# Decay attention and a gated MLP on one core: identity columns beside the keys, mixing from PSUM, double weight pieces, GpSimd relieved, one written order for every engine

## The chip, the cores and the metric

The kernel runs on one core of a Trainium2 chip. The metric is the device time of one execution in microseconds (us). The engines are TensorE (PE for its matmuls, PEld for its weight loads), VectorE (DVE), ScalarE (ACT), GpSimd (POOL) and SyncE (SP, which here only issues DMAs). SBUF is the on-chip memory with 128 partitions, PSUM the one into which matmuls write.

## The reference, cut to what matters

Batch 4, 8 heads, 768 positions, 64 channels a head. The attention has no softmax; it decays by a factor per head and is computed in blocks of 64 positions with a running state. Its output, with the heads laid side by side as 512 channels, goes into a gated MLP whose inputs are mixed with the previous position's.

```python
for b in range(nb):
    sl = slice(b * block, (b + 1) * block)
    qb, kb, vb = (q[:, :, sl], k[:, :, sl], v[:, :, sl])
    intra = np.einsum('bhic,bhjc->bhij', qb, kb) * Dmask[None]
    intra = np.einsum('bhij,bhjd->bhid', intra, vb)
    inter = np.einsum('bhid,bhde->bhie', qb * lam_pow[None], kv_state)
    out[:, :, sl] = intra + inter
    kb_dec = kb * rev_pow[None]
    kv_state = lam_block[None, :, None, None] * kv_state + np.einsum('bhsd,bhse->bhde', kb_dec, vb)
...
xk = mu_k * x + (1.0 - mu_k) * x_prev
xr = mu_r * x + (1.0 - mu_r) * x_prev
k = np.maximum(xk @ w_k, 0.0)
v = k * k @ w_v
r = 1.0 / (1.0 + np.exp(-(xr @ w_r)))
return (r * v).astype(np.float32)
```

`Dmask[i, j]` is the decay to the power i - j (0 above the diagonal), `lam_pow[i]` its power i + 1, `rev_pow[j]` its power 63 - j, `lam_block` its power 64. The weights w_k (512 x 1024), w_v (1024 x 512) and w_r (512 x 512) come as float64.

## The kernel before, in words

The 768 positions are six tiles of 128, two blocks each (`eo` = 0, 1). Heads go in four pairs (`hp`, members `ab`). For each tile and pair:

- `load_hp` loads keys, queries, keys by position, and values, in six DMAs on SP's queue. Queries land in a tile that is zero outside two corners (`Qb`), so that one matmul over 128 rows gives the scores of both heads.
- `attn1` makes the scores (line 155), multiplies them by the decay table `Dt` into `mv` (line 159), and writes queries times `LP` (the decay's powers) into the other half of `mv` (line 172, half of it on DVE, half on GpSimd).
- `attn_state` scales the keys by position (line 182), multiplies them with the values into `u` (line 187) and updates the states, which stand beside the values in `VS` (lines 195 to 205).
- `attn2` multiplies `VS` and `mv` into `xp` (line 220): within-block part and state part in one product, channels on the partitions. ACT copies it to SBUF (line 223), with one column in front for the previous position.
- `prep` mixes it with the previous position, once for r (`which` 1), once for k (`which` 0), on ACT and DVE or ACT and GpSimd, and `split` cuts each mixture into a high part of reduced precision (ACT) and the rest (line 122, on DVE or GpSimd, by a letter in the order).

Each product of the MLP is three matmuls (high by high, high by low, low by high) of 512 columns: `r_slot` has 12 a pair for the four batches, `k_slot` 12 for each eighth of w_k's columns, `v_slot` 12 for half of a batch. A tile has 48 + 96 + 96 of them. `k_slot` then takes the positive part (ACT, line 274), squares it (any engine, line 278) and splits it; `v_slot` multiplies by the sigmoid (line 299) and stores. PSUM has four tiles for r, k and v in turn, two for scores, one for `u` and one for `xp`.

The weights are turned from float64 to two float32 parts on the chip, in 20 pieces of 512 columns: `stage_w` loads a piece, `conv_w` takes the high word's absolute value (ACT, line 139), clamps it (DVE or GpSimd, line 140), shifts it (line 141), ORs in the low word's top bits (line 142) and the sign (line 144), and splits the result. Its scratch tile has four buffers. All of this happens within tile 0.

Two strings set the order in which the steps are written down, `FIRST` for tile 0 and `LATER` for each further tile, whose attention steps belong to the next tile. Letters name steps (L load, A scores, U state, B values, x and y mixtures, R, K, V matmuls, S and C weights). A scheduler may then move the instructions of an engine against each other.

## Time and profile before

| | |
|---|---|
| Median of 3 runs | 468.01 us (465.6 to 468.74) |
| Profiled execution | 468.55 us, of which the span on the core 466.8 us |
| Busy, share of the span | PE 92%, PEld 75%, DVE 57%, ACT 49%, POOL 46% |
| Moved by DMA | 43.00 MB, mean 92 GB/s |
| PE's granted clock, mean | 0.973 |

The profile is of one execution. Busy time is what an engine spent in its instructions; the records of matmuls overlap, and the distance between two starts tells more than the length of one. A float32 matmul shows as two records, each with its own weight load. The chain of waits goes back from the last instruction to whatever released each one. A row of a group gives the output and inputs, the count, the busy time in us and the mean of one in ns, then the idle time of the engine before it.

### The profile page before, as it was taken

How to read it: one execution, taken by the hardware profiler on the slowest of the kernel's cores; microseconds unless marked ns; L12 is line 12 of the kernel's file. 1: busy time of each engine (PE TensorE's matmuls, PEld its weight loads, DVE VectorE, ACT ScalarE, POOL GpSimd, SP SyncE). 2: the span in 40 equal slices, each digit the busy share in tenths (PEclk: the TensorE clock that was granted, in tenths of full speed). 3: DMA queues.
4: the chain of work that ended last, by engine and by line, in shares of the span. 5: the costliest groups of instructions: out<-in, count | busy, mean ns of one | idle time of the engine just before them, and what ended most of it. 6: DMA issues, size and time to landing. Idle time of an engine off the chain costs nothing.

```text
span 466.8 us, 7757 instructions
## 1 busy us (share of the span) xinstructions
PE 430.7 (92%) x3000; PEld 347.8 (75%) x3000; DVE 267.7 (57%) x381; ACT 226.6 (49%) x396; POOL 214.9 (46%) x237
## 2 busy tenths in 40 slices
PE   2597869689889999999999999999999999999997
PEld 2465657567657888888888887888878888888886
DVE  4589999998896415728328546338463266132121
ACT  3376646555483546714546535457335456054410
POOL 4457858756376136925038533145523355121300
PEclk9997979889998999999999999999999999999999
DMA  8899554523123201324004342024142000100011
GB/s 176 241 302 269 162 166 148 165 81 120 72 68 114 70 0 47 112 91 138 22 1 123 104 131 75 22 53 130 67 151 54 0 25 2 69 23 0 1 45 46
DMA packets 22749, 43.00 MB, mean 92 GB/s; under 512 B 4536, under 2 KB 4792, under 8 KB 22712
## 3 DMA queue, kind: packets, MB, share of 16 engines
q1 hardware_dynamic: 19112, 36.20, 26.7%
q10 hardware_dynamic: 3600, 6.29, 3.6%
q8 instruction: 24, 0.39, 0.4%
q14 instruction: 13, 0.11, 0.1%
HBM read 36.19 MB, written 6.30 MB: 91 GB/s over the span
## 4 chain that ended last, share of the span: by engine, by line
PE 71%; DVE 16%; DMA 8%; issue 2%; ACT 2%; SPq 0%; POOL 0%; DVEq 0%; POOLq 0%
PE vp L295 24%; PE kp L271 24%; PE rp L258 12%; PE xp L220 4%; DVE wst L142 3%; PE sc L155 3%; PE u L187 3%; DVE wst L144 2%; DMA qb<-qT 2%; DVE wu L141 2%; DMA wst<-w_r 2%; DVE mv L172 2%; DVE mv L159 2%; DMA kn<-kN 1%; DMA kt<-kT 1%
## 5 line engine op out<-in xcount | busy, mean ns | idle before, releaser
L295 PE MATMUL vp<-wvh,k 128*128 128x512 f32 (+1 forms) x400 | 124.9, 385 | 3.2 <-ACT wvh L121 3.2
L271 PE MATMUL kp<-x,wkh 128*128 128x512 f32 x384 | 126.4, 397 | 1.5 <-ACT wkh L121 1.5
L295 PEld LDWEIGHTS vp<-wvh,k 128*128 128x128 f32 x400 | 74.5, 189 | 18.8 <-ACT wvh L121 3.8
L271 PEld LDWEIGHTS kp<-x,wkh 128*128 128x128 f32 x384 | 72.4, 189 | 18.0 <-ACT wkh L121 1.6
L295 PE MATMUL vp<-wvl,k 128*128 128x512 f32 (+1 forms) x200 | 77.0, 388 | 0.4 <-DVE wvl L122 0.4
L271 PE MATMUL kp<-x,wkl 128*128 128x512 f32 x192 | 75.5, 393 | 0.1
L258 PE MATMUL rp<-wrh,x 128*128 128x512 f32 x192 | 64.5, 408 | 1.8 <-DVE x L122 1.0
L122 POOL TENSOR_TENSOR x<-xt,x 128x512 fp32r<-128x512 f32 x30 | 42.1, 1408 | 28.4 <-ACT x L121 17.8
L241 POOL TENSOR_TENSOR xt<-xt,xt 128x512 f32<-128x512 f32 x24 | 33.0, 1375 | 36.4 <-ACT xt L240 36.1
L220 PE MATMUL xp<-mv,vs 128*64 128x64 f32 (+1 forms) x768 | 38.5, 239 | 11.8 <-DVE vs L197 5.9
L220 PEld LDWEIGHTS xp<-mv,vs 128*64 128x64 f32 (+1 forms) x768 | 31.6, 145 | 22.6 <-DVE vs L197 6.5
L299 DVE TENSOR_TENSOR rt<-vp,rt 128x512 f32<-128x512 f32 (+1 forms) x25 | 16.5, 669 | 52.6 <-PE vp L295 52.4
L274 ACT ACTIVATE kf<-kp 128x512 f32<-128x512 f32 x48 | 28.5, 595 | 35.9 <-PE kp L271 32.8
L258 PEld LDWEIGHTS rp<-wrh,x 128*128 128x128 f32 x192 | 36.7, 193 | 11.8 <-ACT x L121 1.5
L295 PEld LDWEIGHTS vp<-wvl,k 128*128 128x128 f32 x200 | 38.1, 191 | 8.6 <-DVE wvl L122 1.3
L121 ACT CAST k<-kf 128x512 fp32r<-128x512 f32 x48 | 29.8, 620 | 28.9 <-DVE kf L278 17.0
L278 POOL TENSOR_TENSOR kf<-kf 128x512 f32<-128x512 f32 x12 | 12.7, 1058 | 67.6 <-ACT kf L274 67.5
L122 DVE TENSOR_TENSOR k<-kf,k 128x512 fp32r<-128x512 f32 x28 | 20.2, 721 | 41.2 <-ACT k L121 41.1
L278 DVE TENSOR_TENSOR kf<-kf 128x512 f32<-128x512 f32 x22 | 19.6, 892 | 41.5 <-ACT kf L274 41.5
L121 ACT CAST x<-xt 128x512 fp32r<-128x512 f32 x48 | 29.1, 616 | 28.3 <-DVE xt L243 13.7
L271 PEld LDWEIGHTS kp<-x,wkl 128*128 128x128 f32 x192 | 36.3, 189 | 7.9 <-POOL mv L172 0.3
L172 POOL TENSOR_TENSOR mv<-qb,LP 64x256 f32<-64x256 f32 x44 | 35.6, 808 | 12.6 <-PE xp L220 7.6
(56 smaller groups left out, 632.7 us busy)
## 6 DMA issues: line engine op xcount, KB each, us to landing
kt<-kT SPq DMA_DIRECT2D x24, 256.0 KB, 3.9
qb<-qT SPq DMA_DIRECT2D x48, 128.0 KB, 3.5
kn<-kN SPq DMA_DIRECT2D x24, 256.0 KB, 4.0
vs<-vN SPq DMA_DIRECT2D x48, 128.0 KB, 3.4
out<-rt ACTq DMA_DIRECT2D x23, 256.0 KB, 2.1
wst<-w_k SPq DMA_DIRECT2D x8, 512.0 KB, 8.4
wst<-w_v SPq DMA_DIRECT2D x8, 512.0 KB, 3.4
wst<-w_r SPq DMA_DIRECT2D x4, 512.0 KB, 7.5
```

The lines of the kernel that those rows point to most:

```text
L121: nc.scalar.copy(hi, x)
L122: eng.tensor_tensor(lo, x, hi.bitcast(F32), op=ALU.subtract)
L142: nc.vector.scalar_tensor_tensor(lo.bitcast(U32), lo.bitcast(U32), 29, u.bitcast(U32), op0=ALU.logical_shift_right, op1=ALU.bitwise_or)
L172: eng.tensor_tensor(mv[dr, eo, :, ab, :], q[rows, ab, :, eo, :], lp, op=ALU.mult)
L220: nc.tensor.matmul(xp[ab * 64:ab * 64 + 64, b, eo, :], vs[k, eo, b, ab, :], mv[k, eo, b, ab, :], start=True, stop=True)
L241: mix.tensor_tensor(t, t, t2, op=ALU.add)
L258: nc.tensor.matmul(rps[b], x[:, a, b * 128:b * 128 + 128], wr[w][:, hp, :], start=(hp == 0 and i == 0), stop=(hp == HP - 1 and i == 2))
L271: nc.tensor.matmul(p, wk[w][:, hp, f * 128:f * 128 + 128], x[:, a, :], start=(hp == 0 and i == 0), stop=(hp == HP - 1 and i == 2))
L274: nc.scalar.activation(t, p, AF.Relu)
L278: square.tensor_tensor(t, t, t, op=ALU.mult)
L295: nc.tensor.matmul(p[:, cols], k2[f][:, a, b * 128:b * 128 + 128], wv[w][:, f, cols], start=(f == 0 and j == 0), stop=(f == NF - 1 and j = ...
L299: nc.vector.tensor_tensor(o, p[:, cols], o, op=ALU.mult)
```

## The change

**Identity beside the keys.** The host puts a 64 x 64 identity between the keys of a tile's two blocks and joins keys, identity, queries and keys by position into one array. The scores of one head and block are now a matmul of 64 rows, 128 stationary columns (keys and identity) and 64 moving columns (queries): half of the result's partitions hold scores, the other half the queries. The two heads use the upper and the lower 64 rows, and write to two PSUM tiles. `Dt` has the masked decay for the one half and the powers for the other, so that `decay` makes all of `mv` in two instructions of 512 columns. `Qb`, `LP` and line 172 are gone. A pair is loaded in three DMAs.

**Mixes from PSUM.** The copy of `xp` is gone. `mix_prev` (ACT) scales it straight from PSUM for r and for k, shifted by one position, and `mix` (DVE) adds the other share, also from PSUM.

**Weights in pieces of 1024 columns.** Ten pieces instead of twenty; the scratch tile `wu` has one buffer; the clamp is always on GpSimd; bits (`conv_bits`) and split (`conv_split`) are separate steps.

**GpSimd** does the clamps, the clearing of tiles, the columns of the previous position and three powers for the tables. Low parts, mixes and squares are all on DVE. The square of k reads PSUM and the positive part (`k_square`), and two eighths of k are split at once (`k_split`).

**A written order.** One string, `ORDER`, names the steps of all tiles, in smaller steps than before (scores and decay, for instance, are apart), and each engine keeps the order in which the steps stand.

```diff
+class InOrder:
...
+    def __init__(self, tc, engine):
+        self.tc, self.engine = tc, engine
+
+    def __getattr__(self, name):
+        op = getattr(self.engine, name)
+        return lambda *args, **kw: self.tc.keep_in_program_order(op(*args, **kw))
...
     def load_hp(n, hp):
         s = hp % 2
-        kt = work.tile([128, B, 2, 64], F32, name="kt")
-        kn = work.tile([128, B, 2, 64], F32, name="kn")
-        nc.sync.dma_start(kt, kT[n, hp])
-        for ab in range(2):
-            nc.sync.dma_start(Qb[s][ab * 64:ab * 64 + 64, ab], qT[n, hp, ab * 64:ab * 64 + 64])
-        nc.sync.dma_start(kn, kN[n, hp])
+        qks[n, hp] = work.tile([128, 1792], F32, name="qk")
+        sync.dma_start(qks[n, hp], qk[n, hp])
         for eo in range(2):
-            nc.sync.dma_start(VS[s][eo * 64:eo * 64 + 64, eo], vN[n, hp, eo * 64:eo * 64 + 64])
+            sync.dma_start(VS[s][eo * 64:eo * 64 + 64, eo], vN[n, hp, eo * 64:eo * 64 + 64])
...
         if n + 1 < NT:
             if n > 1 or (n == 1 and hp > 1) or (n == 0 and hp < 2):
-                nc.gpsimd.memset(VS[s][64:128, 0], 0.0)
-            nc.gpsimd.memset(VS[s][0:64, 1], 0.0)
-        qkv[n, hp] = (kt, kn)
...
     def tables():
-        nc.sync.dma_start(W[:, 0:64], w0)
-        nc.sync.dma_start(bass.AP(tensor=W.tensor, offset=W.offset + 64, ap=[[128, 8], [4, 16], [1, 4]]), wt)
-        for r in (0, 64):
-            nc.sync.dma_start(
-                Dt[r:r + 64], bass.AP(tensor=W.tensor, offset=W.offset, ap=[[1, 64], [128, 8], [1, 64]]))
-        nc.sync.dma_start(L.rearrange("h (s c) -> (h s) c", c=4), wt)
-        nc.sync.dma_start(
-            LP, bass.AP(tensor=L.tensor, offset=L.offset, ap=[[0, 128], [64, 8], [1, 64]]))
...
+        for eo in range(2):
+            for r in range(2):
+                o, s = (0, H) if r == eo else (64 * H, 0)
+                sync.dma_start(
+                    Dt[r * 64:r * 64 + 64, eo].rearrange("p i h -> p (i h)"),
+                    bass.AP(tensor=W.tensor, offset=W.offset + o, ap=[[s, 64], [1, 64 * H]]))
+
+    def split(hi, lo, x):
+        scalar.copy(hi, x)
+        vector.tensor_tensor(lo, x, hi.bitcast(F32), op=ALU.subtract)
...
+    SLOT = dict(r0=0, r1=1, k0=2, k1=3, k3=0, v0=1, v1=2, v2=3)
+
+    def stage_part(kind, i):
+        slot = SLOT.get(f"{kind}{i}")
+        src = {"r": w_r, "k": w_k, "v": w_v}[kind][i]
         if slot is None:
-            st = work.tile([128, 512, 2], I32, name="wst", bufs=2)
+            t = work.tile([128, 1024, 2], I32, name="wst", bufs=1)
         else:
-            st = big.tile([128, 512, 2], I32, tag=f"big{slot}", name="wst")
-        nc.sync.dma_start(st.rearrange("p c t -> p (c t)"), src.bitcast(I32))
-        return st
-
-    def conv_w(dst, st, clamp, eng, tag):
-        u = work.tile([128, 512], F32, tag=tag, name="wu", bufs=4)
+            t = big.tile([128, 1024, 2], I32, tag=f"big{slot}", name="wst")
+        sync.dma_start(t.rearrange("p c t -> p (c t)"), src.bitcast(I32))
+        st[kind, i] = t
+
...
+    def conv_bits(kind, i):
+        t = st[kind, i]
+        u = work.tile([128, 1024], F32, name="wu", bufs=1)
         ui = u.bitcast(I32)
-        lo, hi = st[:, :, 0], st[:, :, 1]
-        nc.scalar.activation(u, hi.bitcast(F32), AF.Abs)
-        clamp.tensor_single_scalar(u, u, 2.0 ** -15, op=ALU.max)
-        nc.vector.tensor_scalar(ui, ui, 3, 0x3FFFFFF8, op0=ALU.logical_shift_left, op1=ALU.bitwise_and)
-        nc.vector.scalar_tensor_tensor(lo.bitcast(U32), lo.bitcast(U32), 29, u.bitcast(U32),
-                                       op0=ALU.logical_shift_right, op1=ALU.bitwise_or)
-        nc.vector.scalar_tensor_tensor(lo, hi, -0x40000000, lo, op0=ALU.bitwise_and, op1=ALU.bitwise_or)
-        split(dst[0], dst[1], lo.bitcast(F32), eng)
...
+        lo, hi = t[:, :, 0], t[:, :, 1]
+        scalar.activation(u, hi.bitcast(F32), AF.Abs)
+        gpsimd.tensor_single_scalar(u, u, 2.0 ** -15, op=ALU.max)
+        vector.tensor_scalar(ui, ui, 3, 0x3FFFFFF8, op0=ALU.logical_shift_left, op1=ALU.bitwise_and)
+        vector.scalar_tensor_tensor(lo.bitcast(U32), lo.bitcast(U32), 29, u.bitcast(U32),
+                                    op0=ALU.logical_shift_right, op1=ALU.bitwise_or)
+        vector.scalar_tensor_tensor(lo, hi, -0x40000000, lo, op0=ALU.bitwise_and, op1=ALU.bitwise_or)
+
...
+    def conv_split(kind, i):
+        if kind == "k":
+            c, j = i % 2, i // 2
+            dst = [w[:, 2 * c:2 * c + 2, j * 512:j * 512 + 512] for w in wk]
+        else:
+            dst = [w[:, 2 * i:2 * i + 2, :] for w in (wr if kind == "r" else wv)]
+        split(dst[0], dst[1], st.pop((kind, i))[:, :, 0].bitcast(F32).rearrange("p (c o) -> p c o", c=2))
...
+    def scores(n, hp):
...
+        t = qks[n, hp]
+        k = t[:, 0:768].rearrange("p (b j) -> p b j", b=B)
+        q = t[:, 768:1280].rearrange("p (b e i) -> p b e i", b=B, e=2)
+        scs[n, hp] = sc = [ps_s.tile([128, B, 2, 64], F32, tag="sc", name="sc") for ab in range(2)]
         for b in range(B):
             for eo in range(2):
-                nc.tensor.matmul(sc[eo * 64:eo * 64 + 64, b], kt[:, b, eo, :], q[:, :, b, eo, :],
-                                 start=True, stop=True)
-        for eo in range(2):
-            rows = slice(eo * 64, eo * 64 + 64)
-            nc.vector.tensor_tensor(
-                mv[rows, eo].rearrange("p b a i -> p b (a i)"),
-                sc[rows].rearrange("p b a i -> p b (a i)"),
-                Dt[rows, 2 * hp:2 * hp + 2, :].rearrange("p (o a) i -> p o (a i)", o=1).broadcast_to([64, B, 128]),
+                for ab in range(2):
+                    rows = slice(ab * 64, ab * 64 + 64)
+                    tensor.matmul(sc[ab][:, b, eo, :], k[rows, b, eo * 64:eo * 64 + 128], q[rows, b, eo, :],
+                                  start=True, stop=True)
+
+    def decay(n, hp):
+        sc = scs.pop((n, hp))
+        mvs[n, hp] = mv = work.tile([128, 2, B, 2, 64], F32, name="mv")
+        for ab in range(2):
+            vector.tensor_tensor(
+                mv[:, ab].rearrange("p b e i -> p b (e i)"), sc[ab].rearrange("p b e i -> p b (e i)"),
+                Dt[:, :, :, 2 * hp + ab:2 * hp + ab + 1].rearrange("p e i o -> p o (e i)").broadcast_to([128, B, 128]),
                 op=ALU.mult)
+
...
+    def values(n, hp):
+        mv, vs = mvs.pop((n, hp)), VS[hp % 2]
         xp = ps_1.tile([128, B, 2, 64], F32, name="xp")
...
-                    nc.tensor.matmul(xp[ab * 64:ab * 64 + 64, b, eo, :], vs[k, eo, b, ab, :], mv[k, eo, b, ab, :],
-                                     start=True, stop=True)
-        xs = tiny.tile([128, B, 129], F32, name="xs", bufs=3)
-        nc.scalar.copy(xs[:, :, 1:129], xp.rearrange("p b e i -> p b (e i)"))
...
-        t = work.tile([128, B, 128], F32, tag="tmp", name="xt", bufs=4)
-        nc.scalar.activation(t, xs[:, :, 0:128], AF.Copy, scale=omu[:, which, hp:hp + 1])
-        if mix == nc.gpsimd:
-            t2 = work.tile([128, B, 128], F32, tag="tmp", name="xt2", bufs=4)
-            nc.scalar.activation(t2, xs[:, :, 1:129], AF.Copy, scale=mus[:, which, hp:hp + 1])
-            mix.tensor_tensor(t, t, t2, op=ALU.add)
-        else:
-            mix.scalar_tensor_tensor(t, xs[:, :, 1:129], mus[:, which, hp:hp + 1], t,
-                                     op0=ALU.mult, op1=ALU.add)
-        x = xb(n, which, hp)
-        split(x[:, 0, :], x[:, 1, :], t.rearrange("p b i -> p (b i)"), eng)
+                    tensor.matmul(xp[ab * 64:ab * 64 + 64, b, eo, :], vs[k, eo, b, ab, :], mv[k, ab, b, eo, :],
+                                  start=True, stop=True)
+        xps[n, hp] = xp.rearrange("p b e i -> p b (e i)")
...
+    def mix_prev(n, hp):
+        for which in (1, 0):
+            ts[n, which, hp] = t = tiny.tile([128, B, 129], F32, tag=f"ts{which}", name="ts", bufs=4 - 2 * which)
+            scalar.activation(t[:, :, 1:129], xps[n, hp], AF.Copy, scale=omu[:, which, hp:hp + 1])
+            gpsimd.tensor_copy(t[:, :, 0], lastw[:, which, hp, :])
+            if n + 1 < NT:
+                gpsimd.tensor_copy(lastw[:, which, hp, :], t[:, :, 128])
+
+    def mix(n, hp):
+        xp = xps.pop((n, hp))
+        for which in (1, 0):
+            t = ts[n, which, hp]
+            vector.scalar_tensor_tensor(t[:, :, 0:128], xp, mus[:, which, hp:hp + 1], t[:, :, 0:128],
+                                        op0=ALU.mult, op1=ALU.add)
+
+    def split_x(n, which, hp):
+        x = xbuf[which * HP + hp].rearrange("p a (b i) -> p a b i", b=B)
+        split(x[:, 0], x[:, 1], ts.pop((n, which, hp))[:, :, 0:128])
...
+    def k_square(n, f):
+        if f % 2 == 0:
+            kfs[n, f // 2] = work.tile([128, 2, 512], F32, name="kf", bufs=2)
+        p, t = kps.pop((n, f)), kfs[n, f // 2][:, f % 2]
+        scalar.activation(t, p, AF.Relu)
+        vector.tensor_tensor(t, p, t, op=ALU.mult)
+
+    def k_split(n, j):
...
         if n == 0:
...
-            k2.append(big.tile([128, 2, 512], F32R, tag=f"big{f}", name=f"k2_{f}"))
...
-        t = work.tile([128, 512], F32, tag="tmp", name="kf", bufs=4)
-        nc.scalar.activation(t, p, AF.Relu)
-        if square == nc.scalar:
-            square.activation(t, t, AF.Square)
-        else:
-            square.tensor_tensor(t, t, t, op=ALU.mult)
-        split(k2[f][:, 0, :], k2[f][:, 1, :], t, eng)
-
-    vps = {}
-
-    def v_slot(n, i):
+            k2[j] = big.tile([128, 2, 2, 512], F32R, tag=f"big{j}", name=f"k2_{j}")
+        split(k2[j][:, :, 0, :], k2[j][:, :, 1, :], kfs.pop((n, j)))
...
+    for step in ORDER.split():
...
+            i, j = step[1], int(step[2])
+            steps[step[0]](i if i in "rkv" else int(i), j)
...
+ORDER = """
+Sr0 L00 T Cr0 Sr1 k00 U00 T0 u00 A00 a00 L01 A01 Dr0 B00 Cr1 k01 a01 U01 e00 L02 f00 u01 A02 B01 k02 a02 U02 x00 e01
...
+y03 x03 y02 L11 R03 y01 Ck2 k10 Sv0 Dk0 U10 Dk1 Ck3 a10 s00 u10 K00 Sv1 s01 Sv2 K01 k11 B10 s02 Cv0 A11 h00 Dk2 s03
...
+    kT = cut(k)[..., ::-1, :].transpose(3, 1, 2, 6, 0, 4, 5).reshape(NT, HP, 128, B, 2, 64)
+    eye = np.broadcast_to(np.tile(np.eye(64, dtype=np.float32), (2, 1))[:, None], (NT, HP, 128, B, 64))
...
+        "qk": np.concatenate([
+            np.concatenate([kT[:, :, :, :, 0], eye, kT[:, :, :, :, 1]], axis=4).reshape(NT, HP, 128, 768),
```

TensorE, first rows of the program, where the scores of tile 0 stand; before:

```order
L155 MATMUL sc<-qb_90,kt 64x128 x8
L187 MATMUL u<-vs_92,kn 64x128 x8
L220 MATMUL xp<-mv,vs_92 64x64 x16
L155 MATMUL sc<-qb_91,kt 64x128 x8
L187 MATMUL u<-vs_93,kn 64x128 x8
```

and now:

```order
L30 MATMUL u<-vs_92,qk 64x128 x8
L30 MATMUL sc<-qk 128x64 x32
L30 MATMUL xp<-mv,vs_92 64x64 x16
L30 MATMUL u<-vs_93,qk 64x128 x8
L30 MATMUL sc<-qk 128x64 x16
```

The shape is that of the result (partitions x columns). A pair's scores are 16 matmuls of 128 x 64 instead of 8 of 64 x 128; here those of pairs 0 and 1 stand together.

VectorE, just before the first K group's weights are ready; before (wu is the scratch tile, wst a loaded piece, wkl the low part of w_k):

```order
L141 TENSOR_SCALAR wu<-wu 128x512
L172 TENSOR_TENSOR mv<-qb_91,LP 64x4x64
L122 TENSOR_TENSOR wkl<-wst,wkh 128x512
L142 SCALAR_TENSOR_TENSOR wst<-wst,wu 128x512
L197 SCALAR_TENSOR_TENSOR vs_92<-st_94,LP,u 64x4x64 x2
L141 TENSOR_SCALAR wu<-wu 128x512
L144 SCALAR_TENSOR_TENSOR wst<-wst 128x512
L159 TENSOR_TENSOR mv<-sc,Dt 64x512 x2
```

and now:

```order
L30 TENSOR_TENSOR x_87<-ts,x_87 128x512
L30 TENSOR_TENSOR x_91<-ts,x_91 128x512
L30 TENSOR_TENSOR x_86<-ts,x_86 128x512
L30 TENSOR_TENSOR x_85<-ts,x_85 128x512
L30 TENSOR_SCALAR wu<-wu 128x1024
L30 SCALAR_TENSOR_TENSOR wst<-wst,wu 128x1024
L30 SCALAR_TENSOR_TENSOR wst<-wst 128x1024
L30 TENSOR_TENSOR wkl<-wst,wkh 128x2x512 x2
```

Pieces were interleaved with each other, their steps with products of queries and `LP`; now a piece's three bit steps stand together, and the low parts of the first two pieces of w_k stand behind the bits of the third.

305 lines of the change are left out of this document (122 added, 183 removed).

## The prediction

> **What bounds the kernel now.** I read the page first, then busy time by stretch, then the chain of waits in order of time, then the groups by shape.
>
> ```profile
> span 466.8 us, 7757 instructions
> PE 430.7 (92%) x3000; PEld 347.8 (75%) x3000; DVE 267.7 (57%) x381; ACT 226.6 (49%) x396; POOL 214.9 (46%) x237
> ```
>
> No engine but PE is near full on average, but the average hides two stages. In the table by stretch the columns are length, busy time (instructions) of PE, PEld, DVE, ACT, POOL, the granted clock, DMA share and GB/s:
>
> ```profile
> 0.00:40.00 40.00, 22.36 (x220) 17.01 (x220) 26.02 (x43) 18.83 (x36) 20.45 (x29) 0.99 0.91 242
> 40.00:78.00 38.00, 31.85 (x266) 24.35 (x266) 36.96 (x51) 22.97 (x43) 28.79 (x29) 0.84 0.64 190
> 78.00:158.00 80.00, 71.04 (x444) 53.62 (x440) 67.00 (x91) 44.35 (x77) 48.09 (x46) 0.94 0.28 92
> 158.00:224.00 66.00, 66.00 (x473) 54.32 (x470) 34.21 (x52) 33.51 (x59) 32.12 (x38) 1.00 0.26 81
> ```
>
> Up to 40 us the DMA engines are full; from 40 to 78 us DVE is busy 37 of 38 us and PE waits for it, at times at a lower granted clock; from 158 us on PE is busy without a gap at full clock and DVE has 32 of 66 us to spare. The chain of waits (start, length, engine, line) confirms the second stage:
>
> ```profile
> 158.23 11.11 PE kp L271 x48
> ...
> 206.56 1.08 PE xp L220 x32
> 207.65 0.88 PE sc L155 x16
> 208.52 0.87 PE u L187 x16
> ...
> 223.91 11.11 PE kp L271 x48
> ...
> 291.09 11.11 PE kp L271 x48
> ...
> 444.10 19.36 PE vp L295 x108
> ```
>
> The K group of sequence tile 1 starts at 158.23 us, of tile 2 at 223.91, of tile 3 at 291.09: periods of 65.7 and 67.2, mean 66.4. From 158.23 to the end of the last V at 444.10 + 19.36 = 463.46 the chain is 305.2 us of PE work. So there are two prices: whatever shortens the time until the first K group is won in full as long as PE is then fed, and whatever lengthens a PE instruction stream is paid in every period. Work taken from DVE, ACT or GpSimd after 158 us is worth nothing.
>
> **The change part by part.** *Scores.* A head pair's scores were 8 matmuls of 64 stationary and 128 moving columns over all 128 rows (16 records, since each is two passes), 0.88 us. They become 16 matmuls of 128 stationary columns (keys and identity) and 64 moving ones over 64 rows, alternating between the upper and the lower row half: 32 records. What does a record cost when its weight load has 128 columns and little streams past?
>
> ```profile
> L220 PEld LDWEIGHTS xp<-mv,vs x768: 129/138/232, 14.2 to 408.2; 128*64 128x64 f32 x176, 64*64 64x64 f32 x16
> L271 PEld LDWEIGHTS kp<-x,wkl x192: 186/188/330, 71.1 to 443.3; 128*128 128x128 f32 x192
> 460.61 0.42 DVE L299 TENSOR_TENSOR rt<-vp,rt 128x256 f32<-128x256 f32 x1 [2.18 <-PE vp L295]
> 463.49 0.42 DVE L299 TENSOR_TENSOR rt<-vp,rt 128x256 f32<-128x256 f32 x1 [2.45 <-PE vp L295]
> ```
>
> A load of 64 columns lasts 138 ns, one of 128 columns 188 ns (min/median/max). The last two multiplications wait for 24 half-wide matmuls each, all with 128-column loads: 463.49 - 460.61 = 2.88 us, 0.120 us per load-and-matmul. The xp row shows the case with overlap: 32 records, alternating between two column halves, in 1.08 us, 0.034 each, far below the 0.05 by which a load grows with 64 more columns, so the two halves' loads overlap there. Three values for the new scores: as xp, 1.08 us (lower end; a gain below 0.88 is out, since the records double and none streams fewer than 64 columns); the 0.120 us record with the two row halves overlapping as the column halves do, 16 x 0.120 = 1.92; the same with the halves taking turns, 32 x 0.120 = 3.84 (upper end). I take 1.92: the load length is that of the 128-column row, the overlap that of the xp row. That is +1.04 us per pair. Nothing hides it, for PE is the bound. The Trainium skill (TensorE: Matmul & The Clock Gate, "LDWEIGHTS (loading the stationary operand)") says that a load's time follows its columns, at 1.2 per ns, and not its rows; that speaks against this change, since halving the rows saves nothing. The trace's 50 ns for 64 more columns agrees; by that rule with loads strictly one behind another a pair is estimated at 32 x 107 ns = 3.4 us, and the sum below at 486.
>
> *The product of queries and decay* (line 172) goes, since the identity columns put the queries into PSUM and the decay table multiplies them there.
>
> ```profile
> L172 DVE TENSOR_TENSOR mv<-qb,LP 64x256 f32<-64x256 f32 x44 | 35.8, 814 | 6.3 <-DMA qb<-qT 2.7 <-DMA LP<-L 2.4
> L172 POOL TENSOR_TENSOR mv<-qb,LP 64x256 f32<-64x256 f32 x44 | 35.6, 808 | 12.6 <-PE xp L220 7.6 <-DMA LP<-L 2.3 <-DMA qb<-qT 1.1
> L159 DVE TENSOR_TENSOR mv<-sc,Dt 64x512 f32<-64x512 f32 x48 | 33.0, 688 | 13.8 <-PE sc L155 10.0 <-DMA Dt<-W 2.7
> L122 POOL TENSOR_TENSOR x<-xt,x 128x512 fp32r<-128x512 f32 x30 | 42.1, 1408 | 28.4 <-ACT x L121 17.8 <-PE xp L220 10.2
> L241 POOL TENSOR_TENSOR xt<-xt,xt 128x512 f32<-128x512 f32 x24 | 33.0, 1375 | 36.4 <-ACT xt L240 36.1
> ```
>
> The decay stays 48 instructions of 512 columns, now on all partitions; I leave it at 0.69 us. GpSimd's low halves, mixes and squares move to DVE. After the first K group a period then holds about 36 us of DVE work (8 decays, 8 mixes, 8 squares, 4 outputs at 0.69; 16 state updates at 0.48; 8 low halves of x at 0.67; 4 double ones of k at 1.2) in some 70 us: hidden. So is the removed copy of xp on ACT, and so are two new holds: xp's one PSUM tile is now free only after two ACT and two DVE instructions (2 x 0.6 + 2 x 0.69 = 2.6 us instead of 0.6), with the next values group several matmul groups away, and a K tile is free only after DVE's square, with four tiles of 2.8 us in turn. Both are behind DVE's queue, in which the written order lets nothing overtake; its idle half covers that, and if it did not, PE would stand still by the excess in each period.
>
> *Start.* Two piles of DMA and DVE work bound it.
>
> ```profile
> 0.00:10.00 10.00, 1.98 (x16) 1.60 (x16) 4.53 (x12) 3.59 (x6) 5.16 (x12) 1.00 0.84 166
> 10.00:20.00 10.00, 4.15 (x36) 3.13 (x36) 4.67 (x9) 1.91 (x4) 2.38 (x2) 1.00 0.81 237
> 20.00:30.00 10.00, 8.97 (x95) 6.93 (x93) 8.79 (x14) 6.03 (x13) 5.38 (x7) 1.00 1.01 276
> 30.00:40.00 10.00, 7.26 (x78) 5.34 (x76) 8.03 (x10) 7.30 (x14) 7.53 (x9) 0.94 1.01 289
> ```
>
> On SP's queue both w_r pieces (2.10 MB), four head pairs (4 x (0.917 + 0.262) = 4.72 MB, of which the identity is 0.52), the decay table (0.52) and the first w_k piece (1.05) stand ahead of the K work: 8.39 MB. The old kernel had moved 1.66 + 2.37 + 2.76 = 6.79 MB by 30 us; the other 1.60 at 289 GB/s take 5.5: the piece is there at 35.5 us. Fewer, longer DMAs may gain a microsecond, and pair 2 and 3 wait for a buffer each, as before; I count both at nothing. Then the conversions are a chain, because the scratch tile wu has one buffer: each piece's absolute value (ACT), clamp (GpSimd), shift (DVE) and first OR (DVE) must be over before the next piece's absolute value.
>
> ```profile
> L139 ACT ACTIVATE wu<-wst 128x512 f32<-128x512 f32 x20 | 13.4, 674 | 14.1 <-DMA wst<-w_r 12.7 <-DMA wst<-w_v 1.3 <-DVE k L122 0.2
> L140 POOL TENSOR_SCALAR wu<-wu x9: 1481/1492/1931, 13.6 to 133.7; 128x512 f32<-128x512 f32 x9
> L141 DVE TENSOR_SCALAR wu<-wu x20: 411/558/1531, 6.6 to 136.1; 128x512 int32<-128x512 int32 x20
> L142 DVE SCALAR_TENSOR_TENSOR wst<-wst,wu x20: 674/694/3558, 7.1 to 136.6; 128x512 uint32<-128x512 uint32 x20
> L205 DVE SCALAR_TENSOR_TENSOR st<-vs,LP,u 64x256 f32<-64x256 f32 x40 | 19.1, 478 | 1.2
> L299 DVE TENSOR_TENSOR rt<-vp,rt 128x512 f32<-128x512 f32 x23 | 15.6, 690 | 47.9 <-PE vp L295 47.8
> L299 DVE TENSOR_TENSOR rt<-vp,rt 128x256 f32<-128x256 f32 x2 | 0.8, 425 | 4.6 <-PE vp L295 4.6
> L271 PE MATMUL kp<-x,wkh x384: 387/389/797, 71.0 to 443.7; 128*128 128x512 f32 x192
> ```
>
> At 1024 columns: absolute value 1.1, clamp 2.9, shift 0.7, OR 1.2 (the step from 256 to 512 columns, 0.265 us, carried on to 1024), 5.9 and with the hand-overs 6.0 us a piece; if every duration simply doubled, 6.5. In the gaps of this chain DVE does the decays, mixes and x of tile 0, which fit. The third piece's first OR ends at 35.5 + 3 x 6.0 = 53.5, its second at 54.7, the low halves of the first two pieces (2 x 1.2) at 57: the first K group starts at 57 us, where it was 71.0.
>
> From there to the last low halves DVE has 5 conversions (15.5), 6 low halves (7.2), 8 squares and 4 double splits (10.3), 4 decays (2.8), 8 state updates (3.8) and 2 mixes (1.4): 41 us. PE has 144 wide matmuls at 11.11/48 = 0.231 (33.3) and two groups each of scores, u and xp (3.8 + 1.8 + 2.2): also 41. In the old kernel this stretch was 71 to 158 us and DVE-bound (67 of 80 us busy, in part stretched: the OR's median is 0.69, its longest 3.56). Equal piles do not interlock perfectly. The Trainium skill (GPSIMD Engine Reference, "1. Specifications") says that GpSimd shares SBUF interfaces with VectorE and contends with instructions that have two SBUF inputs; the spread from 674 to 3558 ns agrees, and by it the clamps, which stay, would still stretch the ORs and low halves that they meet. I put 4 us, between nothing (perfect interlock) and the 14.5 us of five whole clamps.
>
> *The sum*, against the profiled execution's 466.8 us span (468.55 us in all, 1.75 around it; the median of the runs is 468.01): 57 + one period 66.4 + 305.2 from the second K group to the last V + 3.3 from there to the end of the span (466.8 - 463.46) + 1.75 + 4 = 437.7; scores of the 19 pairs behind the first K group, 19 x 1.04 = 19.8: 457.5. **458 us.** The start wins some 30 us and the scores give 20 back.
>
> **The rivals.** *Scores as quick as xp.* For it: xp's records are as many. Against: their loads are half as wide. 19 x 0.20 instead of 19.8: 442 us.
>
> *The row halves take turns.* Ends on the other side. For it: no matmul of the old kernel uses the lower rows alone, so the overlap is seen for column halves only; 32 x 0.120 = 3.84 us a pair, +56 instead of +20: 494 us. It decides from 2.5 us a pair on: (468 - 458)/19 + 1.92. Against it stands the Trainium skill (TensorE: Matmul & The Clock Gate, "Part 3: Packing small matmuls — row/col tiling"), which has a load overlap running matmuls just where row groups differ; no run here shows it yet.
>
> *The start is not shortened.* Clamps of 3 us on GpSimd in a chain, the DVE work equal to PE's and a fixed order could cost what two-operand GpSimd work cost: first K at 71 as before, 14 later: 472. For it: one scratch tile, no overtaking. Against: DVE's share of the same work falls, and GpSimd's 30 + 24 instructions of 1.4 us are gone. Waits of 3 us in each of five periods would give the same number.
>
> **How the numbers follow.** Forecast 0.55 (its own range 449 to 467: first K group from 53 to 64 us, interlock from 0 to 8, scores from 1.7 to 2.1), scores as xp 0.15, turns 0.15, start not shortened 0.15. The range 438 to 474 leaves out the turns and the ends of the other rivals. A measurement tells about 1% from no change, so faster means under 463.3 and slower over 472.7. Faster: 0.15 + three quarters of 0.55 and a little of the last, 0.60. Slower: 0.15 + four tenths of the last rival, 0.21. Same: 0.19.
>
> **What would show it.** In the new profile: a scores group of 16 matmuls (32 records) about 1.9 us long in the chain of waits between full PE pieces, against 1.1 or 3.8; the first kp near 57 us; PE busy without gaps from there; K groups of tiles 2 and 3 some 70 us apart; the clamp near 2.9 us and the OR's longest well under 3.56. I am wrong if the periods stay at 66 us, if they exceed 75, or if DVE, not PE, stands in the chain after 110 us.

## The result and the profile after

The changed kernel takes 482.12 us in the median (480.80 to 482.64, four runs), the kernel before 468.38 beside it: a ratio of 1.031, with a 95% interval of 1.027 to 1.035. The forecast was 458, with a range up to 474. The prediction was wrong in sign and size. The profiled execution has a span of 480.8 us; by the prediction's sum it should have had 455.75, so 25.1 us have to be found.

The head of the page:

```profile
span 480.8 us, 8110 instructions
PE 457.5 (95%) x3384; PEld 376.8 (78%) x3384; DVE 275.0 (57%) x365; ACT 181.7 (38%) x290; POOL 72.0 (15%) x142
```

GpSimd's load fell from 46% to 15% and ACT's from 49% to 38%, PE's busy time rose by 27 us. (Every instruction of the changed kernel has line 30, the helper that keeps the order, so its rows are told apart by their tiles.) The chain of waits of the changed kernel, in order of time (start, length, engine, tile, records):

```profile
20.12 3.68 PE sc L30 x32
23.80 3.28 PE xp L30 x32
27.08 1.71 PE u L30 x16
...
40.99 3.28 PE xp L30 x32
44.27 5.11 PE rp L30 x12
...
80.94 3.61 PE sc L30 x32
84.55 5.42 PE kp L30 x12
...
116.39 1.08 PE xp L30 x32
...
127.81 1.93 PE sc L30 x32
...
158.87 21.98 PE kp L30 x96
...
226.58 13.82 PE kp L30 x60
...
293.28 21.99 PE kp L30 x96
...
365.03 21.99 PE kp L30 x96
...
455.45 22.10 PE vp L30 x120
```

Late in the program a scores group lasts 1.93 us, as forecast. But from 20 to 44 us the same 32 records take 3.61 (three such groups), u 1.71 instead of 1.02, and PE has no gap there: it runs at half pace. From 80.94 to 89.97 it does so again. The second K group starts at 158.87, the last V ends at 455.45 + 22.10 = 477.55. The table by stretch (columns as in the prediction's):

```profile
20.00:30.00 10.00, 9.88 (x92) 8.64 (x94) 6.72 (x8) 3.26 (x8) 1.41 (x7) 1.00 0.30 93
30.00:40.00 10.00, 10.00 (x98) 8.73 (x96) 6.26 (x10) 4.72 (x10) 1.08 (x5) 1.00 0.47 138
...
80.00:90.00 10.00, 10.00 (x62) 8.15 (x62) 9.80 (x11) 3.89 (x5) 6.22 (x7) 0.51 0.38 131
```

The slow stretch of 80 to 90 us shows a granted clock of 0.51. That of 20 to 40 us shows 1.00, with the same 3.61 us a group: the column doesn't show the first slow stretch. There PE is full, while DVE is at two thirds and the DMA engines, full in the kernel before at that time, at a third to a half. The first matmul of the first K group, from the instructions in order of time:

```profile
69.97 0.50 PE L30 MATMUL kp<-x,wkh 128*128 128x512 f32 x1
```

So the account, term by term, in us of the profiled execution:

| Term of the sum | predicted | measured | difference |
|---|---|---|---|
| start of the first K group | 57 | 69.97 | +13.0 |
| from there to the second K group (66.4 + 4 x 1.04 + 4) | 74.6 | 88.90 | +14.3 |
| from there to the last V's end (305.2 + 15 x 1.04) | 320.8 | 318.68 | -2.1 |
| from there to the span's end | 3.3 | 3.25 | -0.1 |

### The profile page after: what moved, and what is told of

Read it like the earlier page. It is cut to its first block, busy times and chain, and to the rows that moved or that the text cites. A ratio compares the mean times of both kernels' runs of the same rounds, so it can differ in the third digit from the quotient of the medians.

```text
span 480.8 us, 8110 instructions
## 1 busy us (share of the span) xinstructions
PE 457.5 (95%) x3384; PEld 376.8 (78%) x3384; DVE 275.0 (57%) x365; ACT 181.7 (38%) x290; POOL 72.0 (15%) x142
## 4 chain that ended last, share of the span: by engine, by line
PE 90%; DVE 3%; DMA 3%; POOL 2%; issue 1%; ACT 0%; SPq 0%; POOLq 0%; ACTq 0%
PE vp L30 28%; PE kp L30 27%; PE rp L30 13%; PE sc L30 10%; PE xp L30 7%; PE u L30 5%; DMA qk<-qk 2%; POOL wu L30 1%; DVE wst L30 1%; DMA W<-PW 1%; DVE x L30 1%; DVE wu L30 1%; SPq L30 0%; DVE mv L30 0%; DMA smalls<-small 0%
## 5 line engine op out<-in xcount | busy, mean ns | idle before, releaser
L30 PE MATMUL kp<-x,wkh 128*128 128x512 f32 x384 | 122.8, 397 | 0.0
L30 DVE TENSOR_TENSOR mv<-sc,Dt 128x512 f32<-128x512 f32 x48 | 52.3, 1131 | 30.9 <-PE sc L30 30.8
L30 DVE TENSOR_TENSOR kf<-kp,kf 128x512 f32<-128x512 f32 x48 | 33.0, 688 | 51.8 <-ACT kf L30 51.7
L30 PEld LDWEIGHTS sc<-qk 64*128 64x128 f32 x768 | 52.9, 217 | 11.2 <-issue 5.2
L30 PE MATMUL sc<-qk 64*128 64x64 f32 x768 | 56.4, 305 | 4.8 <-DMA qk<-qk 4.8
L30 ACT ACTIVATE ts<-xp,omu 128x512 f32<-128x512 f32 x48 | 30.3, 684 | 45.0 <-PE xp L30 40.9
L30 DVE SCALAR_TENSOR_TENSOR ts<-xp,smalls,ts 128x512 f32<-128x512 f32 x48 | 33.8, 746 | 23.2 <-ACT ts L30 22.0
L30 ACT CAST x<-ts 128x512 fp32r<-128x512 f32 x48 | 28.2, 618 | 38.1 <-DVE rt L30 24.5
L30 PE MATMUL xp<-mv,vs 128*64 128x64 f32 (+1 forms) x768 | 36.9, 242 | 2.1 <-DVE mv L30 1.4
L30 PE MATMUL rp<-wrl,x 128*128 128x512 f32 x96 | 38.8, 405 | 0.0
```

The source lines that it names most:

```text
L30: return lambda *args, **kw: self.tc.keep_in_program_order(op(*args, **kw))
```

## The experiments

Three theories were set against each other for the first two terms. *Sleeping TensorE*: PE ran at half pace because attention's small matmuls alone never brought it to full pace. *Order*: one scratch tile and waits kept in the written order delay the conversions. *Table*: a decay lasts 1.13 us instead of 0.69, because in the new table consecutive elements of a head stand eight elements apart. And one experiment asks what the scores' price hangs on.

**Long matmuls to keep PE busy.** Float32 matmuls of 128 x 512 on a tile of ones, whose result nobody reads (Z):

```diff
-... L01 A01 Dr0 B00 Cr1 k01 a01 U01 e00 L02 f00 u01 A02 B01 ...
+... L01 Z05 A01 Z01 Dr0 B00 Z01 Cr1 k01 a01 U01 Z01 e00 L02 f00 u01 A02 Z01 B01 Z01 ...
```

> Adds work that computes nothing of the output: wide float32 matmuls (128 x 512, on a tile of ones) on TensorE, five ahead of the scores of pair 1 and one behind each following attention group up to the first R group. Theory, TensorE cold: in the changed kernel TensorE ran 28 us without a gap (20 to 48 us) at half pace on small matmuls alone; wide ones bring it to full pace. Then scores, xp and u last 1.9, 1.1 and 1.0 us instead of 3.6, 3.3 and 1.7 from pair 1 on, which saves about 13 us less some 6 us of added matmuls, the first K group starts at 58 to 64 us instead of 70, and the time is about 472 us (0.98 of the changed kernel's 482, 1.01 of the kernel before). Rival, the chain of the conversions (one scratch tile, waits in the written order): TensorE gets quick but the K group still starts at 68 or later, and the time stays within 3 us of 482. Third possibility: the dummies do not change the pace, and the time grows by their own 6 us to 488.

Measured: 479.31 us, ratio to the kernel before 1.027 [1.022, 1.032]. Scores lasted 1.93 us from pair 1 on, so the pace is a matter of what PE did before. (Of the 28 us in the changed kernel the last 4.4, from 44.2 on, are the first R products, not small ones.) But each added matmul took 1.05 us on PE's path, and the first K group started at 67.6. The dose hid the effect.

**The table made dense.** ScalarE copies it once, with the head outermost:

```diff
-    Dt = const.tile([128, 2, 64, H], F32, name="Dt")
+    Dt = const.tile([128, H, 2, 64], F32, name="Dt")
...
+        scalar.copy(Dt, raw.rearrange("p e i h -> p h e i"))
```

(The states of the first pair, `u00`, also move ahead of the table's loads in `ORDER`.)

> The decay table is put into SBUF with the head outermost, so that the decay reads consecutive elements instead of every eighth one; ScalarE copies it once. Theory, the stride of the table is what makes a decay 1131 ns instead of 688: the decay falls to about 0.69 us, DVE gets 0.44 us x 12 = 5.3 us back before the second K group, and the time falls by 3 to 6 us (476 to 479). Rival, PSUM or the full 128 partitions make it slow: 1.1 us as before, time unchanged. By the theory of the cold TensorE the first K group starts no more than 3 us earlier.

Measured: 477.82 us, 1.025 [1.017, 1.033]. The group of decays (busy time, mean ns of one, idle time before), first of the changed kernel, then of this one:

```profile
L30 DVE TENSOR_TENSOR mv<-sc,Dt 128x512 f32<-128x512 f32 x48 | 52.3, 1131 | 30.9 <-PE sc L30 30.8
```

```profile
L30 DVE TENSOR_TENSOR mv<-sc,Dt 128x512 f32<-128x512 f32 x48 | 30.8, 684 | 34.0 <-PE sc L30 31.3 <-ACT Dt L30 2.7
```

The stride was the whole of it: 1131 to 684 ns. But the first K group started at 69.3, some 0.6 us earlier, and the time is that of the next kernel, which keeps the strided table. Both lack the drop of the clock at 80 us, which the last experiments price at 4 us; so the table is worth about nothing here.

**More scratch.** For w_k's first three pieces:

```diff
-        u = work.tile([128, 1024], F32, name="wu", bufs=1)
+        kf = kind == "k" and i < 3
+        u = work.tile([128, 1024], F32, tag="kf" if kf else "wu", name="wu", bufs=2 if kf else 1)
```

> The scratch tile of the first three w_k pieces' conversions takes two more buffers (those of kf, which are idle then), so that a piece no longer waits for the piece ahead. Theory of the cold TensorE: the absolute values stand on ScalarE behind the mixes, which wait for a slow TensorE, so the K group starts less than 3 us earlier and the time stays within 3 us of 482. Rival, the scratch chain: the pieces overlap, the first K group starts at about 62 instead of 70 us, and the time is about 474.

Measured: 478.19 us, 1.025 [1.019, 1.030], first K group at 69.8. The scratch tile is not what holds the K group of the changed kernel; the four microseconds gained go with the missing drop of the clock (granted 1.00 from 80 to 90 us, 0.51 in the changed kernel).

**The identity once.** Four matmuls with 64 identity columns carry all queries of a pair (256 moving columns each); the 16 of the keys have 64 stationary columns:

```diff
+        for eo in range(2):
+            for ab in range(2):
+                rows, lo, hi = slice(ab * 64, ab * 64 + 64), eo * 64, 64 - eo * 64
+                tensor.matmul(sc[ab][hi:hi + 64, :, eo, :], k[rows, 0, 64:128], q[rows, :, eo, :],
+                              start=True, stop=True)
...
-                    tensor.matmul(sc[ab][:, b, eo, :], k[rows, b, eo * 64:eo * 64 + 128], q[rows, b, eo, :],
+                    tensor.matmul(sc[ab][lo:lo + 64, b, eo, :], k[rows, b, eo * 128:eo * 128 + 64], q[rows, b, eo, :],
```

> The identity is no longer loaded beside the keys of every matmul: for each head and block one matmul with 64 identity columns carries the queries of all four batches (256 moving columns), and the 16 score matmuls of a pair have 64 stationary columns. Theory, the scores' price is the width of their loads: the group falls from 1.93 us to 1.3 (16 key matmuls as xp, 1.08, and four of 0.22 that overlap) to 1.96 (they do not overlap); at 1.4 the time falls by 19 x 0.5 = 10 us to about 472. Rival, the price is the number of records or the row halves: the group stays at 1.9 or more, and the time at 482 or above.

Measured: 455.86 us, 0.977 [0.970, 0.983]: quicker than both kernels. The chain of waits and the scores' instructions of this kernel, and the latter of the changed kernel (min/median/max in ns):

```profile
19.62 1.99 PE sc L30 x40
21.61 3.08 PE xp L30 x32
...
168.21 1.06 PE sc L30 x40
```

```profile
L30 PEld LDWEIGHTS sc<-qk x960: 128/135/228, 11.7 to 384.2; 64*64 64x64 f32 x192
```

```profile
L30 PEld LDWEIGHTS sc<-qk x768: 182/188/335, 11.7 to 408.1; 64*128 64x128 f32 x192
```

Forty records now take 1.06 us where 32 took 1.93: neither the number of records nor the row halves are the price, but the 128 columns that each load brings, 188 ns instead of 135. (Loads of 64 columns can also alternate between column halves, as those of xp do; what of the gain is the shorter load and what this overlap, the run doesn't separate.) For the 13 scores groups behind the second K group that is 13 x 0.87 = 11.3 us; that stretch fell by 10.3. The start is still slow (1.99 and 3.08), but three short scores groups save 5 us of it: the first K group is at 64.6.

**Short matmuls, once.** The reduced type of the MLP's products, twelve in a row, where PE waits for a load:

```diff
-... u00 A00 a00 L01 A01 Dr0 B00 ...
+... u00 A00 a00 L01 Z12 A01 Dr0 B00 ...
```

> Added work that the output does not use: twelve short matmuls (128 x 512, the reduced type of the MLP's products, about 0.23 us each at full pace) in a row on TensorE ahead of the scores of pair 1, in time in which TensorE waits; nothing after that. If only waking counts, scores, xp and u of pairs 1 to 3 then last 1.9, 1.1 and 1.0 us and the first R group starts at 36 to 40 us (44.3 in the changed kernel). If small matmuls alone do not hold the pace, they fall back to 3.6, 3.3 and 1.7 within a few us.

Measured: 466.9 us in its single run, 15 less than the changed kernel. The chain of waits:

```profile
11.85 3.61 PE sc L30 x32
15.46 4.57 PE wp L30 x12
20.04 1.93 PE sc L30 x32
```

Before the twelve a scores group lasts 3.61 us, behind them 1.93, and it stays so. The first K group starts at 58.2, where 57 was forecast. Sleeping TensorE was the 12 us by which the changed kernel is later.

**One behind each group too.** Z01 behind each attention group up to the first R group, as in the first experiment, but of the short kind.

> The same twelve ahead of the scores of pair 1, and one of 0.23 us behind each of the following attention groups up to the first R group (some 2 us in all; in the run with long ones each cost 1.05 us, 14 us in all). Theory, the cold TensorE alone makes the start late: full pace up to R, the first R group at 36 to 38 us, the first K group at 60 to 63 us instead of 70, the time 472 to 475. Rival, the weights of w_k stand on the DMA queue behind loads that wait for TensorE, and their conversions behind mixes and in a chain: R is early, but the K group moves by less than the R group does, to 65 or later, and the time is 477 or more.

Measured: 472.62 us, 1.011 [1.009, 1.014]; first R group at 37.29, first K group at 60.3. The start and the time that the theory gave, but the clock fell from 70 to 80 us (granted 0.50), which brings the next question.

**Order alone**, and **order with the short matmuls**. The loads of w_k's first two pieces stand ahead of those of pairs 2 and 3, the bits of its first three ahead of the mixes:

```diff
-f01 L03 A03 Sk0 u02 Sk1 B02 Dr1 x01 y00 k03 R00 e02 a03 f02 U03 Ck0 u03 Sk2 B03 e03 f03 Sk3 x02 L10 R01 R02 A10 Ck1
-y03 x03 y02 L11 R03 y01 Ck2 k10 Sv0 Dk0 U10 Dk1 Ck3
+f01 Ck0 L03 A03 u02 B02 Dr1 x01 y00 k03 R00 Ck1 e02 a03 f02 U03 u03 Sk2 B03 Ck2 e03 f03 Sk3 x02 L10 R01 R02 A10
+y03 x03 y02 L11 R03 y01 k10 Sv0 Dk0 U10 Dk1 Ck3
```

(Sk0 and Sk1 stand in the row above, behind L01 and L02.)

> Order alone: the loads of the first two w_k pieces are written ahead of those of pairs 2 and 3, and the bits of the first three w_k pieces ahead of the mixes of pairs 1, 2 and 3. Theory, the written order makes the start late (the first piece landed at 40 us and its absolute value began at 45.5, against 35.5 in the prediction): the pieces land by 30 us, the third first OR is over by 55, and the first K group starts at 60 to 64 us; the time is 473 to 477. Rival, the cold TensorE: R groups and mixes are as late as before, the K group waits for the low halves of x instead, it starts at 67 or later, and the time stays within 3 us of 482.

> Both: the early order and the short matmuls that keep TensorE at pace. If the order and the pace each hold up the K group, so that mending one leaves the other, the first K group starts at 52 to 58 us, which is the predicted start, and the time is 465 to 470. If the DVE's work ahead of it is the bound, the K group starts at 62 or later in this one as in the two single ones.

Measured: 476.37 us (1.019 [1.016, 1.021]) with the first K group at 70.3, and 471.58 (1.009 [1.007, 1.011]) with it at 66.6. The first K group of this order is no earlier than the changed kernel's, so order as the cause falls, as far as one other order can show it. That its time still lies in the range of the order theory (473 to 477) is luck: it too lacks the drop of the clock (granted 1.00 from 70 to 120 us). Nor did the two add up. In the second the chain of waits shows why:

```profile
20.67 2.00 PE sc L30 x32
...
26.83 7.69 DMA qk<-qk
34.65 2.27 PE sc L30 x32
...
37.64 3.28 PE xp L30 x32
```

Weights that go first make the last pair's load land at 34.5 us; PE waits for it for 1.2 us, and behind the wait its xp is slow again.

**Once, timed**, with the same edit, and **what wakes PE**: 24 float32 matmuls of 64 stationary and 128 moving columns instead of the twelve.

> The kernel with twelve short matmuls once, timed: its single run gave 466.9 us with the first K group at 58.2. If waking TensorE before 20 us is the whole difference, the median is 465 to 468.5 and the ratio to the kernel before is 0.995 to 1.003; if the single run was lucky, it lies between 470 and 476, where the kernel with a dummy behind each group lay.

> What wakes TensorE: instead of twelve matmuls of 128 x 512, 24 float32 ones in the shape of the old scores and of u (64 stationary and 128 moving columns over 128 rows, about 0.23 us each at half pace, 5.5 us in all), at the same place. In the kernel before, 3.9 us of scores and u of that shape in a row stood ahead of the first ones at full pace. If unbroken work with 128 moving columns suffices, scores of pair 1 last 1.9 us and the time is about 467; if only 512 columns or the reduced type do, they last 3.6, the first R group starts at 44 or later, and the time is about 482.

Measured: 470.80 us (470.52 to 474.73), 1.011 [1.005, 1.017], and 471.3 in a single run. The timed kernel lies in the range that was to show luck, and the two profiled executions of it say what the luck was. Both start the first K group alike, at 58.2 and 58.3, with gaps alike; by stretch, first the single run, then the timed one:

```profile
60.00:70.00 10.00, 7.89 (x77) 6.05 (x77) 9.05 (x12) 5.11 (x8) 5.34 (x4) 1.00 0.77 304
70.00:80.00 10.00, 10.00 (x62) 8.03 (x61) 9.87 (x10) 5.05 (x7) 5.17 (x6) 1.00 0.48 183
```

```profile
60.00:70.00 10.00, 7.88 (x60) 5.89 (x58) 9.05 (x12) 5.27 (x8) 4.91 (x4) 0.90 0.71 297
70.00:80.00 10.00, 10.00 (x59) 8.01 (x58) 9.87 (x10) 5.39 (x7) 5.49 (x6) 0.59 0.38 132
```

Behind 2.1 us of waiting between 60 and 70 us the clock was halved in the one and not in the other, and their second K groups start at 147.23 and 143.24: the drop costs some 4 us. The narrow matmuls woke PE as the wide ones did (scores of pair 1 at 23.16, lasting 1.93), only later, after 7.6 us of them; the first K group started at 62.6. So, in this single run, float32 work of 128 moving columns over all rows is enough, and the type and width of the MLP's products aren't needed. What it is in attention's groups that does not wake PE (64 moving columns, scores on half the rows, the mixture) was not separated.

**Filling the gaps around the first K group** with twice six short matmuls, and then **keeping PE awake all along**: those, the twelve, and one behind each group.

```diff
-y03 x03 y02 L11 R03 y01 ... K01 k11 B10 s02
+y03 x03 y02 L11 F06 R03 y01 ... K01 k11 F06 B10 s02
```

> The kernel with twelve short matmuls ahead of the scores of pair 1, and two more groups of six (the output does not use them) in the two places where TensorE waits for VectorE around the first K group: ahead of the last R product of tile 0 and ahead of the xp group behind the second kp group. If gaps of two to three microseconds are what halves the clock for up to ten, the clock stays at 1.00 from 66 to 80 us, the stretch from the first to the second K group is 85 us (88.9 with the drop), and the median is 466 to 468 instead of 470.8. If the drop has another cause, the time is 471 to 473.

> Added matmuls that the output does not use: twelve ahead of the scores of pair 1, one behind each attention group up to R, and six in each of the two gaps around the first K group. If the two drops of the clock are worth 12 and 4 us, and the added ones cost some 3 us on TensorE's path, the first K group starts at 59 to 61, the second 85 us later, and the time is 467 to 470: what is then left of the 24 us is attention that the new order puts behind the first K group. If the time stays at 472 or more, the second drop is not worth 4 us.

Measured: 472.54 us (467.36 to 472.86), 1.010 [1.004, 1.016], and 469.51 (469.13 to 470.68), 1.006 [1.004, 1.009]. In the former the fill worked where it stood (granted 1.00 from 50 us on, 85.3 us from the first to the second K group, 88.9 in the changed kernel), but PE fell asleep at about 29 us, so its time lies where "another cause" was to show. One of its four runs, with a mean granted clock of 0.999, took 467.36. In the latter the clock no longer dropped (mean 0.999 to 1.000 in all ten runs):

```profile
70.00:80.00 10.00, 9.75 (x99) 8.13 (x100) 9.74 (x12) 4.77 (x7) 6.25 (x8) 1.00 0.31 98
```

Its first K group starts at 61.0, 2.8 later than with twelve alone (the matmuls that fill in), its second 85.2 later. So a PE that is always awake makes the changed kernel 12.6 us quicker even with these matmuls in its way, and no quicker than the kernel before. What then is missing from 458 isn't the clock.

**The two edits together**, identity once and PE awake:

> The identity once per head and block, and the twelve short matmuls. If the two causes add up, the three slow pairs of the former (scores 1.92 instead of 1.06, xp 3.08 instead of 2.11, u 1.71 instead of 0.88: 2.7 a pair) give 8 us: 446 to 450. If DVE, 96 hundredths busy from 60 to 110 us, is next behind them, less than 4 us is won: 452 or more.

> The same with the dense decay table. If DVE bounds the stretch from the first to the second K group once TensorE is awake and its scores are short, the 22 decays up to there (8 and 14) give up to 0.44 x 14 = 6 us more than without: 440 to 445. If TensorE bounds it, the time is within 2 us of the kernel without.

> The same dummies on the kernel with the identity once per head and block. There the clock was halved from 67 to 71 us: if the fill prevents that, 450 to 452 instead of 452.8; otherwise 453 to 455.

> The same on the kernel with the identity once per head and block: with the clock at full pace throughout, 449 to 452 us and a narrower spread than with twelve alone (452.4 to 459.6); if VectorE bounds the stretch up to 110 us, no better than 453.

Measured: with the twelve 452.81 us (0.969 [0.965, 0.973]), the quickest kernel of the study; with the dense table 456.13 (0.977 [0.971, 0.982]); with the gaps filled 455.29 (0.975 [0.971, 0.978]); with a matmul behind each group 456.93 (0.977 [0.971, 0.983]). The additions won nothing, and the twelve only 3 us of the 8 expected. That is the outcome that was named for VectorE as the next bound, and the chains of waits agree. Of the kernel with twelve short matmuls, once:

```profile
44.69 2.78 POOL wu L30
...
108.58 0.77 DVE ts L30
...
110.14 1.15 PE xp L30 x32
```

Between these pieces the chain holds no work of PE: from 44 to 109 us it runs on DVE, GpSimd's clamps and ACT. It does so up to 109.06 in the quickest kernel and up to 113.13 with PE always awake. So with the clock full DVE's stream, with the clamps in it, is the bound until then, and a quicker PE wins nothing there. It is not the whole of the missing 5 us: in the profiled executions the first K group moved from 64.6 to 57.5, but that of the kernel with the identity once was the slowest of its four (458.68, the others 453.33 to 455.94), and where the others gained isn't known.

In the profiled executions with the dense table and with a matmul behind each group PE was slow again between 20 and 40 us (granted 0.79 and 0.70, 0.55 and 0.93 in the two tens). That quicker scores leave gaps there which the slow ones covered is a guess that no run tests. The single runs of these kernels lie between 452 and 461 us, and how often the clock drops where in them was not settled.

## Why the prediction was wrong

**The scores: right.** 1.93 us a group, forecast 1.92: row halves overlap, and the load of 128 columns sets the length. The rivals at 1.08 and 3.84 fall. There are 19 groups behind the first K group, as counted. The periods, which were to be some 70 us, are 67.7 and 66.7 (226.58 - 158.87, 293.28 - 226.58): by the prediction's own test that speaks against the scores' price, but the test was blunt, since a period holds as many groups as the order puts there. These two hold three scores groups each, the next one four, and that is 71.75 us long (365.03 - 293.28).

**GpSimd without two-operand work: right in size, for a reason of its own.** The clamp's mean is 3.03 us for 2.9 forecast. The OR no longer stretches (min/median/max in ns, changed kernel):

```profile
L30 DVE SCALAR_TENSOR_TENSOR wst<-wst,wu x10: 1225/1226/1227, 12.6 to 109.9; 128x1024 uint32<-128x1024 uint32 x10
```

The longest OR of the kernel before had 3.56 us for half as many columns. But the prediction also said that the clamps, which stay, would stretch the ORs that they meet, and here no OR meets one: with one scratch tile a clamp comes only after the OR ahead of it. In the kernel with more scratch two ORs fall into a clamp, and they take 1.93 and 1.94 us:

```profile
L30 DVE SCALAR_TENSOR_TENSOR wst<-wst,wu x10: 1225/1226/1940, 12.5 to 107.4; 128x1024 uint32<-128x1024 uint32 x10
```

The low halves of w_k do meet clamps in the changed kernel; the longest takes 2.06 us where 1.2 was forecast, and the longest clamp 3.76.

**The start: the failed step.** The prediction took the start for "a chain, because the scratch tile wu has one buffer", fed by a piece that is there at 35.5 us, with the waits of pairs 2 and 3 for a buffer counted "at nothing". It gave PE's own work ahead of the first K group no term at all. In the changed kernel PE was the bound from 20 to 53 us, most of it at half pace, and the rest waited in line behind it. On the DMA queue and on ACT, in order of time:

```profile
35.30 1.10 SPq L30 DMA_DIRECT2D vs<-vN  x2
36.46 3.28 SPq L30 DMA_DIRECT2D wst<-w_k  x4
```

```profile
44.31 1.27 ACT L30 ACTIVATE ts<-xp,omu 128x512 f32<-128x512 f32 x2 [3.21 <-PE xp L30]
45.47 1.17 ACT L30 ACTIVATE wu<-wst 128x1024 f32<-128x1024 f32 x1
```

The last pair's values got their buffer at 35.30, and only then were the four w_k pieces issued; the first absolute value stands on ACT behind a mix that waited for xp, at 45.47 where the sum had 35.5. With PE awake (twelve short matmuls, once) the first K group starts at 58.2, so the 12 us were PE's:

```profile
36.27 1.15 ACT L30 ACTIVATE wu<-wst 128x1024 f32<-128x1024 f32 x1 [0.22 <-DMA wst<-w_k]
54.98 1.23 DVE L30 SCALAR_TENSOR_TENSOR wst<-wst,wu 128x1024 uint32<-128x1024 uint32 x1
57.39 3.19 DVE L30 TENSOR_TENSOR wkl<-wst,wkh 128x1024 fp32r<-128x1024 f32 x2
58.16 0.49 PE L30 MATMUL kp<-x,wkh 128*128 128x512 f32 x1
```

That 58.2 is so near to 57 is in part luck. The first piece is there at 36.3 for 35.5, but the third piece's first OR is over at 56.2 for 53.5, and the two low halves at 60.6 for 57: 6.6 us a piece, not 6.0. The K group doesn't wait for both low halves, as the sum had it; it starts behind the last R products and a u group. The trace of the kernel before had shown PE at half pace, and what ended it:

```profile
18.30 3.01 PE L220 MATMUL xp<-mv,vs 128*64 128x64 f32 x28 [3.64 <-POOL mv L172]
21.64 1.98 PE L155 MATMUL sc<-qb,kt 128*64 128x128 f32 x16 [0.33 <-DMA qb<-qT]
23.46 1.93 PE L187 MATMUL u<-vs,kn 128*64 128x128 f32 x16
```

Behind the scores and u of 128 moving columns in a row, 3.8 us, the next scores took 1.09. The change makes the scores' moving side 64 columns, so no such row is left. The rival "the start is not shortened" had the right place and even the first K group at 71, but its reason, waits in the chain, isn't the one that the runs show.

The Trainium skill (TensorE: Matmul & The Clock Gate, "Part 1: The HAM clock gate (the 'warmup' mystery)") says that TensorE starts at half rate and is released by about 3.4 us of sustained activity, and falls back after about as long a window of idleness. Here 24 us of attention groups without a gap (20.1 to 44.2) didn't release it, with 64 moving columns in the scores and xp and single u groups between them; the R products behind them did. In the kernel before, PE was at pace behind 3.8 us of 128 moving columns. And 2.1 us of waiting, in pieces of at most 0.8, were enough for a drop, in one of two executions. That fits the page's statement that the window runs free of the kernel, not the length of idleness that it asks for.

**From the first to the second K group: two terms missing.** Four of the 14.3 us are the second drop of the clock (88.9 with it, 84.1 to 85.3 without it in the kernels of the same order, scores and table). Most of the rest is a seam in the sum: it put the old periods behind a start that the new order had emptied. The scores' instructions by stretch, of the kernel before and of the changed one (from the first to the second K group, and on to the last V):

```profile
71.00:158.23 87.23, 5.78 (x62) 4.33 (x62) 5.50 (x8) 0.94 0.31 99
158.23:463.46 305.23, 14.35 (x195) 11.23 (x194) 19.27 (x28) 1.00 0.19 61
```

```profile
69.97:158.87 88.90, 13.69 (x192) 12.81 (x192) 15.36 (x14) 0.94 0.36 125
158.87:477.55 318.68, 26.03 (x416) 24.23 (x416) 28.66 (x26) 1.00 0.18 62
```

At 16 records a pair the kernel before had 4 groups in this stretch and 12 behind it, so 8 of the 24 ahead of it; at 32 a pair the changed kernel has 6 and 13, so 5 ahead. The sum counted 1.04 us for each of the 19, but the whole of a group only for four in the stretch. Two further groups of scores, u and xp (2 x (1.93 + 1.02 + 1.08)) are 8.1 us. The old periods that it took hold 37 and 65 records of scores, so rather three groups than four: another 0.8. 4.0 + 8.1 + 0.8 is 12.9 of the 14.3; some 1.4 us of the stretch stay unassigned.

**Behind the second K group: a near hit of two errors.** The sum had 15 increments of 1.04, 15.6 us; the stretch grew by 13.5 (318.68 - 305.23). It holds 13 scores groups for 12, but 13 u groups for 14 (208 and 224 records) and 14 xp groups for 15 (448 and 480). 13 x 1.93 - 12 x 0.88, less one u and one xp (1.02 and 1.08), is 12.4 us, 3.2 less than the sum had; 1.0 more stays unassigned.

**The interlock: right in size.** The prediction had piles of 41 us for DVE and PE and 4 for their waits, 45 from the first K group to the last low halves. In the kernel with twelve short matmuls, once, it is 46.2 (58.16 to 104.37), with no work of PE in the chain of waits. In the changed kernel PE idled for 2.1 us from the first to the second K group; DVE was full there too (8.8 to 9.9 of every 10 us from 60 to 120), but with PE at half pace from 80.94 to 89.97 the chain runs on PE from 79 us on. (The prediction's list of a later period's DVE work adds up to 37 us, not 36; nothing hangs on it.)

**The decay: wrong, and free.** "I leave it at 0.69 us" was 1.13, 21 us of DVE time in all; the dense table took it away and won nothing that could be told from the drop of the clock. From the first to the second K group it is 83.4 us with the dense table and 84.1 in the kernel with more scratch, both without a drop.

With the clock always full and its price for that taken off (469.51 - 2.8 = 466.7), some 9 us remain to 458: 1.2 of the first K group (58.2 for 57) and 10.6 of the stretch behind it (85.2 for 74.6: the further groups, a little more interlock, and what is unassigned), less the 2.1 behind the second K group. The last us lies in the rounding and between that profiled execution and the median.
